# Three of four block sums moved from GpSimd to VectorE in a Strassen-like mixture-of-experts stage, with later output DMAs and a re-spaced start of the stage

## The chip, the cores and the metric

The kernel runs on one core of a Trainium2 chip. The core has five engines with a queue each: TensorE (PE, matmuls; PEld is its weight load), VectorE (DVE), ScalarE (ACT), GpSimd (POOL) and SyncE (SP, which here only issues DMAs). Every queue is worked off in order: an instruction that waits holds up all that stand behind it on its engine, and only there. The metric is the device time of one execution in microseconds (us); lower is better.

## The reference

Windowed attention, then a feed-forward block with a rational activation, then a mixture of 8 experts whose gate is normalised by 8 rounds of row and column scaling.

```python
x = attention(q, k, v)                    # (4, 8, 576, 64) -> (2304, 512)
h = x @ w_in                              # (2304, 2048)
x = rational(h, a, b) @ w_out             # (2304, 512)
logits = x @ w_gate                       # (2304, 8)
P = np.exp(logits - logits.max())
for _ in range(8):
    P /= P.sum(1, keepdims=True) + 1e-09
    P /= P.sum(0, keepdims=True) + 1e-09
    P *= N / E
for e in range(8):
    h = np.maximum(x @ w1[e], 0.0)        # w1[e]: (512, 1024)
    out += P[:, e:e + 1] * (h @ w2[e])    # w2[e]: (1024, 512)
```

## The kernel before

All arithmetic is float32 in effect: each matrix is split into a high and a low float16 part, and each product is three float16 matmuls (high-high, high-low, low-high).

The expert stage takes about two thirds of the time, and the change lies in it. Both of its matrix products are computed with seven block products in place of eight. The tokens are three groups G of 768, each of two blocks of 384. A **macro** m is one expert, one token group and one of `NP` = 4 pairs of 128 hidden columns: 8 x 3 x 4 = 96 macros. A macro's first layer is seven **units** (`moe_unit`, positions 0 to 6, position 1 seven units late), each six matmuls of 128x384. Their sums leave PSUM as they come up: positions 0, 2 and 4 by ACT copies (L973), position 3 by a DVE add (L975) and an ACT relu (L976), position 5 by a DVE add (L978), position 6 by an ACT relu (L980), position 1 by a DVE add (L983) and an ACT relu over two blocks (L984). These evacuations matter: positions 0, 2, 4 and 6 add into one PSUM bank (`l1a`), so PE may not start position 2 before L973 has read position 0, and so on; positions 3, 5 and 1 share the bank `l1b` in the same way with L975, L978 and L983.

After the four blocks of h (the tile E) come **four sums of blocks** (the tile D in room IG), written by `combine` (L946): o = 6 is E1 - E0 and needs only position 6's relu; o = 4, 5 and 7 come after L984, and 5 needs 4, and 7 needs 5. Before, a macro with m < 4 makes all four on DVE, every other macro makes all four on GpSimd. Then E[1:4] (1152 columns) and D (1536 columns) are each split: the high part by ACT (L990), the low part by DVE (L991), two of each in a macro. From here on "first" L990 or L991 is the one of E, "second" the one of D.

The second layer (`moe_l2`) lags by `LG` = 28 units; in every unit three of its products run (nine matmuls of 128x256, L1013 to L1015) between the units of the first layer. A finished piece is summed out of PSUM by one ACT copy (L1032) and seven DVE adds (L1034), scaled by the gate on ACT (L1043, twice), and added to the output in HBM by a DMA that GpSimd issues (L1048; for expert 0 SP issues a plain one).

The weights of the next expert are prepared meanwhile: loaded into two buffers by SP (L838, L844 to L846), their maximum taken on DVE (L850), four differences made on GpSimd (L873; for expert 0 on DVE), and split by ACT (L884) and DVE (L887). The gate's rounds (`gate_iter`) are nine small DVE operations and one tiny matmul that waits for them; group 2 of x is cut and stored by `mix_at` near the start of the stage.

What sets the order: the code places work at units (`at_u`, `prep_at`, `mix_at`), and a scheduler then orders each engine's queue by its own estimates. `pin` adds a dependency that keeps a GpSimd or other instruction behind the last named sum or split.

Of the kernel before, what the change touches and what calls it, by code (L numbers as in the profile page):

```python
# [16 lines left out]
ALU = mybir.AluOpType  # L17
# [11 lines left out]
def kernel(  # L29
# [14 lines left out]
    nc = tc.nc  # L44
# [199 lines left out]
    for i, x in enumerate(SEAMS):  # L244
        if x is None:
            continue
        m = masks[:, i, 0:32 + x]
# [430 lines left out]
    def rat_c(st):  # L678
        d = cur[st]
        g = d.pop("g")  # L680
        gh, gl = (slab_g[:, x + st % 2, :] for x in (0, 2))
        nc.scalar.activation(gh, g, AF.Copy)  # L682
        nc.gpsimd.tensor_tensor(out=gl, in0=g, in1=gh.bitcast(F32), op=ALU.subtract)  # L683
        d.update(gh=gh, gl=gl)
# [132 lines left out]
    NP = NF2 // 2  # L817
# [10 lines left out]
    def pin(eng, i):  # L828
        if eng in behind:
            tc.add_manual_dep(i.ins, behind[eng], mybir.DependencyInfo(mybir.DependencyClass.Sync, mybir.DependencyReason.DATA), reason="after this group's h")  # L830
# [111 lines left out]
    def combine(m, o, x, y, op):  # L942
        d = mac[m]
        a, b = (d["E"][:, z, :] if z < 4 else d["D"][:, z - 4, :] for z in (x, y))
        eng = nc.vector if m < NP else nc.gpsimd
        i = eng.tensor_tensor(out=d["D"][:, o - 4, :], in0=a, in1=b, op=op)  # L946
        if m >= NP:
            behind["p"] = i.ins.name

    def moe_unit(u):  # L950
# [41 lines left out]

    yb = {}
    pend = []
    gate_ready = [False]
    PRODS = ((0, 0, 1, 0), (0, 1, 5, 4), (1, 0, 4, 3), (1, 1, 6, 5), (2, 0, 3, 1), (2, 1, 7, 2), (3, 0, 2, 6))
    NQ = NM * 3 * 7
# [21 lines left out]
    def gate_col(e, tt):  # L1019
        if (e, "pw") not in pw:  # L1020
            pwt = cpool.tile([P, NTT], F32, tag=f"pw{e % 2}", name="pwt")
            nc.vector.tensor_scalar(out=pwt, in0=gate_t["pe"][:, e, :], scalar1=i_e[:, e % 2:e % 2 + 1], scalar2=None, op0=ALU.mult)
            pw[e, "pw"] = pwt
        return pw[e, "pw"][:, tt:tt + 1]
# [15 lines left out]
    def y_out(v, p, yd):  # L1040
        e, G = GV[v]
        for n in range(2):
            nc.scalar.activation(yd[:, n, :], yd[:, n, :], AF.Copy, scale=gate_col(e, 2 * TPB * G + TPB * n + p))  # L1043
        dst = bass.AP(out.tensor, (2 * TPB * G + p) * P * DM, [[DM, P], [TPB * P * DM, 2], [1, DM]])
        if e == 0:
            nc.sync.dma_start(out=dst, in_=yd)
        else:
            nc.gpsimd.dma_start(out=dst, in_=yd, accum_op=ALU.add)  # L1048

    def flush_pend():  # L1050
        gate_ready[0] = True
        for a in pend:
            y_out(*a)
        pend.clear()
# [57 lines left out]
    def at(s, fn, *a):  # L1112
        slots[s].append((fn, a))
# [12 lines left out]
    def at_u(u, fn, *a):  # L1126
        at(4 * NS1 + int(2 * u), fn, *a)
# [10 lines left out]
    def mix_at(G, when, s0, slot0):  # L1138
        for dt, c, slot in zip(s0, (CX00, CX10, CT1, CX11, CT2, CT3, CT4), (0, 1, 2, 3, 0, 1, 2)):
            if c in (CT1, CT2, CT3, CT4):  # L1140
                when(dt, mix_sub, G, c)
            when(dt, mix_put, G, c, slot0 + slot)
            if c == CX11:
                when(dt + (0.5 if G < 2 else 2), x2_logits, G)
# [3 lines left out]

    mix_at(0, at_step, (56, 57, 58, 59, 61, 62, 63), 0)
    mix_at(1, at_step, (69, 70, 71, 72, 74, 75, 76), 0)  # L1150
    mix_at(2, at_u, (9.5, 11, 12.5, 14, 29, 31, 33), 4)
    for c in range(7):
        at_step(78 + c // 3, x_load, 0, c)
    at_step(80.5, x_load, 1, CX00)

    at_u(20.5, gate_exp)
    for u in (23, 25.5, 31, 35, 38, 42, 45, 49):
        at_u(u, gate_iter)
    at_u(50, gate_done)
    at_u(50.5, flush_pend)  # L1160

    use = []

# [4 lines left out]
    def prep_at(s, e, k, step):  # L1168
        for n in range(4):
            at(int(s + n * step), raw_diff, e, k, n)  # L1170
        for n in range(4):
            at(int(s + (1, 2, 4, 5)[n] * step), raw_part, e, k)
        use.append((int(s + 5 * step), e, k, s))

    US = 4 * NS1
# [5 lines left out]
        prep_at(4 * x + 1, 0, i, 1)  # L1181
    for i, x in ((0, 90), (3, 92), (1, 94)):
        prep_at(4 * x + 1, 0, NP + i, 1)
    prep_at(US + 2 * 16, 0, NP + 2, 1)
    for e in range(1, NE):
        u0 = EU * (e - 1)
        for i in range(8):
# [12 lines left out]
    def run_slot(s):  # L1200
        for fn, a in slots.pop(s, ()):
            early = fn is run_piece or fn is flush
            with tc.high_priority(offset=400) if early else ExitStack():
                more = fn(*a)
            if callable(more):
                at(s + 1, more)
# [78 lines left out]
        run_slot(4 * g + 3)  # L1285
    side_mode[0] = 1
    for u in range(NU + LG):
        if u == LG:
            side_mode[0] = 2
        if u == 0:  # L1290
            rat_b(NS1 - 1)
        moe_unit(u)
        run_slot(US + 2 * u)
        if u < 2 * LAG:
            rat_l2(NS1 - LAG + u // 2, u % 2)
        if u == 1:
            rat_c(NS1 - 1)
        for q in range(3 * (u - LG), 3 * (u - LG + 1)):
            if 0 <= q < NQ:
                moe_l2(q)  # L1300
        run_slot(US + 2 * u + 1)
    assert not slots


# [28 lines left out]
```

## Time and profile before

| | us |
|---|---|
| median of 3 runs (lowest, highest) | 2087.18 (2082.1, 2087.22) |
| the profiled execution | 2087.59 |
| its span, first to last instruction | 2085.8 |
| busy in the span: PE, DVE, ACT, POOL | 1914.8, 1515.0, 1229.1, 944.9 |

A busy time is the sum over stages with different limits, and PE's matmuls are pipelined, so a busy PE is not a PE at its peak. Idle time of an engine costs the kernel something only where PE, or the end, waits for what that engine does next.

### The profile page before, as it was taken

The page shows a single profiled execution, that of the slowest core. Times are in us where ns is not written, and L with a number is a line of the kernel's source. Part 1 is how long each engine was busy: PE and PEld are TensorE (multiplying, and loading weights), DVE is VectorE, ACT ScalarE, POOL GpSimd, SP SyncE. Part 2 cuts the span into 40 slices and gives each one's busy share as a digit, 9 for nine tenths or more (in the row PEclk, how much of TensorE's full clock was granted, in tenths as well). Part 3 has the DMA queues.
Part 4 walks back from the last instruction along what each step waited for, and adds up shares of the span by engine and source line. Part 5 has one row for each costly group of instructions (what it writes and reads, how often), then busy time and mean ns, then how long its engine had stood idle before and what let it go on. Part 6 is the DMA issues. An engine that isn't in the chain of part 4 may idle for free. (4 is left out here: it accounts for less than half of the span.)

```text
span 2085.8 us, 36459 instructions
## 1 busy us (share of the span) xinstructions
PE 1914.8 (92%) x13914; PEld 1433.3 (69%) x13914; DVE 1515.0 (73%) x2572; ACT 1229.1 (59%) x2328; POOL 944.9 (45%) x846
## 2 busy tenths in 40 slices
PE   7688999998989899999999999999999999999997
PEld 6466767776766566767677677677677667767776
DVE  5898899899998776667576666666666666666653
ACT  5677777685777345545554654654555455455542
POOL 1232333221221036546564763665566476475542
PEclk7699999998999899999999999999999999999999
DMA  6542220134211251344245345345435524633323
GB/s 170 160 139 77 59 70 12 35 99 130 84 39 54 68 171 61 104 129 107 59 125 147 64 111 155 72 99 129 105 59 125 159 60 104 160 75 71 79 61 49
DMA packets 209792, 200.07 MB, mean 96 GB/s; under 512 B 78288, under 2 KB 160208, under 8 KB 209616
## 3 DMA queue, kind: packets, MB, share of 16 engines
q1 hardware_dynamic: 192480, 164.70, 26.0%
q0 software_dynamic: 17136, 33.03, 10.6%
q8 instruction: 109, 1.79, 0.4%
q14 instruction: 67, 0.55, 0.1%
HBM read 151.67 MB, written 46.01 MB: 95 GB/s over the span
## 5 line engine op out<-in xcount | busy, mean ns | idle before, releaser
L924 PEld LDWEIGHTS <-roomA 128*128 128x128 f16 x3276 | 320.9, 98 | 223.1 <-issue 59.2
L924 PE MATMUL l1a<-roomA 128*128 128x384 f16 x1872 | 358.3, 327 | 28.5 <-ACT roomA L973 16.8
L924 PE MATMUL l1b<-roomA 128*128 128x384 f16 x1404 | 274.4, 330 | 14.5 <-DVE roomV L978 5.3
L683 POOL TENSOR_TENSOR roomIG<-roomA,roomIG 128x384 fp32r<-128x384 f32 x96 | 112.5, 1172 | 290.4 <-ACT roomIG L682 222.2
L946 POOL TENSOR_TENSOR roomIG<-roomV 128x384 f32<-128x384 f32 x92 | 112.8, 1227 | 262.6 <-ACT roomV L980 112.8
L873 POOL TENSOR_TENSOR roomA<-roomA 128x256 f32<-128x256 f32 x224 | 211.2, 962 | 22.3 <-DVE roomA L887 8.4
L946 POOL TENSOR_TENSOR roomIG<-roomA 128x384 f32<-128x384 f32 x92 | 110.4, 1200 | 195.2 <-ACT roomA L980 99.4
L1013 PE MATMUL yps<-roomA 128*128 128x256 f16 x630 | 170.9, 273 | 7.0 <-ACT roomA L884 2.7
L1013 PE MATMUL yps<-roomA,roomV 128*128 128x256 f16 x630 | 171.6, 275 | 2.4 <-DVE roomA L1034 1.5
L1014 PE MATMUL yps<-roomA,roomV 128*128 128x256 f16 x630 | 172.1, 275 | 0.0
L1015 PE MATMUL yps<-roomA 128*128 128x256 f16 x630 | 170.6, 274 | 1.0 <-DVE roomA L991 1.0
L1015 PE MATMUL yps<-roomA,roomV 128*128 128x256 f16 x630 | 170.3, 275 | 1.3 <-DVE roomV L991 1.3
L1014 PE MATMUL yps<-roomA 128*128 128x256 f16 x630 | 171.4, 273 | 0.0
L645 PE MATMUL h1ps<-roomA 128*128 128x384 f16 x384 | 130.6, 341 | 16.4 <-DVE roomA L665 8.2
L991 DVE TENSOR_TENSOR roomV<-roomIG,roomV 128x1536 f16<-128x1536 f32 x48 | 87.6, 1825 | 79.2 <-ACT roomV L990 79.2
L887 DVE SCALAR_TENSOR_TENSOR roomA<-roomA,sm 128x768 f16<-128x768 f32 (+1 forms) x92 | 123.8, 1355 | 28.3 <-ACT roomA L884 27.6
L991 DVE TENSOR_TENSOR roomA<-roomIG,roomA 128x1536 f16<-128x1536 f32 x48 | 94.2, 1962 | 68.0 <-ACT roomA L990 68.0
L698 PE MATMUL o1ps<-roomIG,roomV 128*128 128x384 f32 x384 | 137.6, 358 | 4.2 <-POOL roomIG L683 4.1
L884 ACT ACTIVATE roomA<-roomA,sm 128x768 f16<-128x768 f32 (+1 forms) x92 | 94.5, 1037 | 79.7 <-POOL roomA L873 50.7
L699 PE MATMUL o1ps<-roomIG,roomV 128*128 128x384 f32 x384 | 131.3, 342 | 0.0
L646 PE MATMUL h1ps<-roomA 128*128 128x384 f16 x384 | 130.0, 339 | 0.0
L647 PE MATMUL h1ps<-roomA 128*128 128x384 f16 x384 | 129.7, 338 | 0.0
(216 smaller groups left out, 5240.9 us busy)
## 6 DMA issues: line engine op xcount, KB each, us to landing
roomA<-xd SPq DMA_DIRECT2D x119, 384.0 KB
roomA<-in_moe_w_dram SPq DMA_DIRECT2D x256, 128.0 KB
roomA<-in_moe_w_dram SPq DMA_DIRECT2D x128, 256.0 KB
out_dram<-roomV POOLq DMA_DIRECT2D x32, 512.0 KB, 5.8
out_dram<-roomA POOLq DMA_DIRECT2D x31, 512.0 KB, 6.1
roomV<-in_moe_w_in_dram SPq DMA_DIRECT2D x16, 512.0 KB
roomA<-in_moe_w_out_dram SPq DMA_DIRECT2D x16, 512.0 KB
xd<-roomA SPq DMA_DIRECT2D x14, 384.0 KB
```

The lines of the kernel that those rows point to most:

```text
L645: mm = nc.tensor.matmul(hp, whi, xb[:, 0, kk, :], start=kk == 0, stop=False)
L646: nc.tensor.matmul(hp, whi, xb[:, 1, kk, :], start=False, stop=False)
L647: nc.tensor.matmul(hp, wlo, xb[:, 0, kk, :], start=False, stop=kk == KD - 1)
L698: nc.tensor.matmul(ob[dd], hi, d["gl"], start=False, stop=False)
L699: nc.tensor.matmul(ob[dd], lo, d["gh"], start=False, stop=last)
L873: pin("p" if e else "v", eng.tensor_tensor(out=d[:, o, :], in0=a, in1=b, op=ALU.add if w == 0 and n == 0 else ALU.subtract))
L924: mm = nc.tensor.matmul(ps, w[:, wx_, wh, kk * P:(kk + 1) * P], x[:, xh, kk, :], start=start and kk == 0 and wh == 0 and xh == 0, stop=sto ...
L946: i = eng.tensor_tensor(out=d["D"][:, o - 4, :], in0=a, in1=b, op=op)
L991: behind["v"] = nc.vector.tensor_tensor(out=h[:, 1, o, :], in0=src, in1=h[:, 0, o, :], op=ALU.subtract).ins.name
L1013: nc.tensor.matmul(o, hh[:, a - 1, c], w[:, m, 0, :], start=i == 0 and half == 0, stop=False)
L1014: nc.tensor.matmul(o, hh[:, a - 1, c], w[:, m, 1, :], start=False, stop=False)
L1015: nc.tensor.matmul(o, hl[:, a - 1, c], w[:, m, 0, :], start=False, stop=i == NP - 1 and (half == 1 or b == 3))
```

## The change

Four things. `combine` puts only o = 6 on GpSimd, for every macro, and o = 4, 5 and 7 on DVE. The output DMAs on GpSimd (experts 1 to 7) are issued two units later in the program than the scaling before them, and pinned behind the last o = 6. The work at the start of the stage is placed at other units: the seven cuts of group 2, the gate's exponential (20.5 to 23.5), its eight rounds (from 23, 25.5, 31, 35, 38, 42, 45, 49 to one every three units from 26 to 47), its end and the held-back outputs, and one weight preparation of expert 0 (unit 16 to 23). Nothing else is edited, but the scheduler orders all queues anew.

```diff
--- before.py
+++ after.py
@@ -942,9 +942,9 @@
     def combine(m, o, x, y, op):
         d = mac[m]
         a, b = (d["E"][:, z, :] if z < 4 else d["D"][:, z - 4, :] for z in (x, y))
-        eng = nc.vector if m < NP else nc.gpsimd
+        eng = nc.gpsimd if o == 6 else nc.vector
         i = eng.tensor_tensor(out=d["D"][:, o - 4, :], in0=a, in1=b, op=op)
-        if m >= NP:
+        if o == 6:
             behind["p"] = i.ins.name
 
     def moe_unit(u):
@@ -992,6 +992,8 @@
 
     yb = {}
     pend = []
+    later_u = []
+    unit_now = [0]
     gate_ready = [False]
     PRODS = ((0, 0, 1, 0), (0, 1, 5, 4), (1, 0, 4, 3), (1, 1, 6, 5), (2, 0, 3, 1), (2, 1, 7, 2), (3, 0, 2, 6))
     NQ = NM * 3 * 7
@@ -1045,7 +1047,7 @@
         if e == 0:
             nc.sync.dma_start(out=dst, in_=yd)
         else:
-            nc.gpsimd.dma_start(out=dst, in_=yd, accum_op=ALU.add)
+            later_u.append((unit_now[0] + 2, lambda: pin("p", nc.gpsimd.dma_start(out=dst, in_=yd, accum_op=ALU.add))))
 
     def flush_pend():
         gate_ready[0] = True
@@ -1148,16 +1150,16 @@
 
     mix_at(0, at_step, (56, 57, 58, 59, 61, 62, 63), 0)
     mix_at(1, at_step, (69, 70, 71, 72, 74, 75, 76), 0)
-    mix_at(2, at_u, (9.5, 11, 12.5, 14, 29, 31, 33), 4)
+    mix_at(2, at_u, (9, 12, 15.5, 19, 27.5, 30, 32.5), 4)
     for c in range(7):
         at_step(78 + c // 3, x_load, 0, c)
     at_step(80.5, x_load, 1, CX00)
 
-    at_u(20.5, gate_exp)
-    for u in (23, 25.5, 31, 35, 38, 42, 45, 49):
+    at_u(23.5, gate_exp)
+    for u in (26, 29, 32, 35, 38, 41, 44, 47):
         at_u(u, gate_iter)
-    at_u(50, gate_done)
-    at_u(50.5, flush_pend)
+    at_u(49, gate_done)
+    at_u(49.5, flush_pend)
 
     use = []
 
@@ -1181,7 +1183,7 @@
         prep_at(4 * x + 1, 0, i, 1)
     for i, x in ((0, 90), (3, 92), (1, 94)):
         prep_at(4 * x + 1, 0, NP + i, 1)
-    prep_at(US + 2 * 16, 0, NP + 2, 1)
+    prep_at(US + 2 * 23, 0, NP + 2, 1)
     for e in range(1, NE):
         u0 = EU * (e - 1)
         for i in range(8):
@@ -1285,6 +1287,9 @@
         run_slot(4 * g + 3)
     side_mode[0] = 1
     for u in range(NU + LG):
+        unit_now[0] = u
+        while later_u and later_u[0][0] <= u:
+            later_u.pop(0)[1]()
         if u == LG:
             side_mode[0] = 2
         if u == 0:
@@ -1299,6 +1304,8 @@
             if 0 <= q < NQ:
                 moe_l2(q)
         run_slot(US + 2 * u + 1)
+    for _, fn in later_u:
+        fn()
     assert not slots
```

Lines from L994 on are two higher in the changed kernel, from L1048 on a few more; L1034 becomes L1036, L1043 becomes L1045, L1048 becomes L1050.

First place: DVE in the macro m = 66 (expert 5), from one second L991 to the next; roomV_6583 and roomA hold the blocks E of two macros, roomIG holds D. Before:

```order
L978 TENSOR_TENSOR roomV_6583<-l1b,roomV_6583 128x384
L850 TENSOR_REDUCE sm<-roomA 128x1 x2
L200 TENSOR_REDUCE sm<-sm 128x1
L850 TENSOR_REDUCE sm<-roomA 128x1
L983 TENSOR_TENSOR roomV_6583<-l1b,roomV_6583 128x384
L975 TENSOR_TENSOR roomA<-l1b,roomA 128x384
L991 TENSOR_TENSOR roomV_6693<-roomV_6583,roomV_6693 128x1152
L991 TENSOR_TENSOR roomV_6693<-roomIG,roomV_6693 128x1536
```

In the changed kernel:

```order
L1036 TENSOR_TENSOR roomA<-yps,roomA 128x256
L978 TENSOR_TENSOR roomV_6583<-l1b,roomV_6583 128x384
L975 TENSOR_TENSOR roomA<-l1b,roomA 128x384
L850 TENSOR_REDUCE sm<-roomA 128x1 x2
L200 TENSOR_REDUCE sm<-sm 128x1
L983 TENSOR_TENSOR roomV_6583<-l1b,roomV_6583 128x384
L850 TENSOR_REDUCE sm<-roomA 128x1
L946 TENSOR_TENSOR roomIG<-roomV_6583 128x384
L991 TENSOR_TENSOR roomV_6693<-roomV_6583,roomV_6693 128x1152
L946 TENSOR_TENSOR roomIG<-roomIG,roomV_6583 128x384
L946 TENSOR_TENSOR roomIG<-roomV_6583,roomIG 128x384
L991 TENSOR_TENSOR roomV_6693<-roomIG,roomV_6693 128x1536
```

L978 and L975 now stand ahead of the maxima L850, L983 stands ahead of the third L850 where it stood behind it, and the three sums stand one ahead of the first L991 and two behind it.

The same macro on ACT, before:

```order
L1043 ACTIVATE roomA<-roomA,pwt 128x512 x2
L973 ACTIVATE roomV_6583<-l1a 128x384
L973 ACTIVATE roomA<-l1a 128x384
L980 ACTIVATE roomV_6583<-l1a 128x384
L984 ACTIVATE roomV_6583<-roomV_6583 128x768
L973 ACTIVATE roomA<-l1a 128x384
L990 ACTIVATE roomV_6693<-roomV_6583 128x1152
L976 ACTIVATE roomA<-roomA 128x384
L990 ACTIVATE roomV_6693<-roomIG 128x1536
```

In the changed kernel:

```order
L973 ACTIVATE roomA<-l1a 128x384
L973 ACTIVATE roomV_6583<-l1a 128x384
L1045 ACTIVATE roomA<-roomA,pwt 128x512 x2
L976 ACTIVATE roomA<-roomA 128x384
L980 ACTIVATE roomV_6583<-l1a 128x384
L984 ACTIVATE roomV_6583<-roomV_6583 128x768
L990 ACTIVATE roomV_6693<-roomV_6583 128x1152
L973 ACTIVATE roomA<-l1a 128x384
L990 ACTIVATE roomV_6693<-roomIG 128x1536
```

Both have the second L990 at the end with an L973 between L984 and it; the next macro's L973 stands behind it in both.

Second place: GpSimd at the end of macro 64, in 65 and at the start of 66. Before:

```order
L946 TENSOR_TENSOR roomIG<-roomIG,roomV_6583 128x384
L946 TENSOR_TENSOR roomIG<-roomV_6583,roomIG 128x384
L1048 DMA out_dram<-roomV_6583 128x2x512
L946 TENSOR_TENSOR roomIG<-roomA 128x384 x2
L946 TENSOR_TENSOR roomIG<-roomIG,roomA 128x384
L946 TENSOR_TENSOR roomIG<-roomA,roomIG 128x384
L1048 DMA out_dram<-roomA 128x2x512
L946 TENSOR_TENSOR roomIG<-roomV_6583 128x384 x2
```

In the changed kernel, where a macro fills one row, macros 64 to 68:

```order
L1050 DMA out_dram<-roomA 128x2x512
L873 TENSOR_TENSOR roomA<-roomA 128x256 x4
L946 TENSOR_TENSOR roomIG<-roomV_6583 128x384
L1050 DMA out_dram<-roomV_6583 128x2x512
L946 TENSOR_TENSOR roomIG<-roomA 128x384
L1050 DMA out_dram<-roomA 128x2x512
L946 TENSOR_TENSOR roomIG<-roomV_6583 128x384
L946 TENSOR_TENSOR roomIG<-roomA 128x384
L1050 DMA out_dram<-roomV_6583 128x2x512
L946 TENSOR_TENSOR roomIG<-roomV_6583 128x384
```

A macro has one sum in place of four, and an output DMA stands between sums as before, two units later.

Third place: DVE in the macro m = 3, the last before the second layer begins; gt and gs are the gate's tiles, smps its tiny matmul's. Before:

```order
L787 TENSOR_REDUCE gs<-gt 128x18
L946 TENSOR_TENSOR roomIG<-roomA 128x384 x2
L788 TENSOR_SCALAR gs<-gs 128x18
L946 TENSOR_TENSOR roomIG<-roomIG,roomA 128x384
L789 RECIPROCAL gs<-gs 128x18
L975 TENSOR_TENSOR roomA<-l1b,roomA 128x384
L946 TENSOR_TENSOR roomIG<-roomA,roomIG 128x384
L790 TENSOR_TENSOR gt<-gt,gs 128x144
L792 TENSOR_REDUCE gs<-gt 128x8
L991 TENSOR_TENSOR roomA<-roomIG,roomA 128x1536
```

In the changed kernel, its first twelve rows:

```order
L787 TENSOR_REDUCE gs<-gt 128x18
L873 TENSOR_TENSOR roomA<-roomA 128x256 x2
L887 SCALAR_TENSOR_TENSOR roomA<-roomA,sm 128x3x256
L946 TENSOR_TENSOR roomIG<-roomA 128x384
L788 TENSOR_SCALAR gs<-gs 128x18
L873 TENSOR_TENSOR roomA<-roomA 128x256
L946 TENSOR_TENSOR roomIG<-roomIG,roomA 128x384
L789 RECIPROCAL gs<-gs 128x18
L873 TENSOR_TENSOR roomA<-roomA 128x256
L975 TENSOR_TENSOR roomA<-l1b,roomA 128x384
L946 TENSOR_TENSOR roomIG<-roomA,roomIG 128x384
L790 TENSOR_TENSOR gt<-gt,gs 128x144
```

One sum has left, and four differences and one split of expert 0's weights have come in ahead of L975.

## Rows read from the trace of the kernel before

**Rows 1.** Stretches: busy us (count) of PE, PEld, DVE, ACT, POOL; PEclk, DMA, GB/s.

```profile
676.00:704.00 28.00, 17.61 (x82) 9.75 (x82) 25.03 (x50) 14.10 (x21) 0.00 (x0) 0.71 0.41 127
760.00:840.00 80.00, 75.02 (x558) 55.17 (x556) 55.91 (x84) 44.44 (x64) 47.84 (x41) 0.98 0.30 94
840.00:1956.00 1116.00, 1063.27 (x8020) 783.20 (x8018) 732.48 (x1025) 607.41 (x884) 658.57 (x564) 1.00 0.43 106
```

**Rows 2.** Waits of PE, 840 to 1956: waited for, us in total, times, longest.

```profile
PE l1a L924 <- ACT roomA L973: 15.6, 18, 2.3
PE l1a L924 <- ACT roomV L973: 13.6, 22, 0.9
PE l1b L924 <- DVE roomV L978: 6.9, 8, 0.9
PE yps L1013 <- DVE roomA L1034: 5.4, 10, 0.9
PE yps L1013 <- DVE roomV L1034: 4.2, 7, 0.9
PE yps L1013 <- ACT roomA L884: 2.7, 5, 0.6
```

**Rows 3.** Timeline around macro 66: start, us, operation, [idle before <- releaser].

```profile
1631.15 1.22 DVE L850 TENSOR_REDUCE sm<-roomA 128x1 f32<-128x1024 f32 x1 [5.58 <-DMA roomA<-in_moe_w_dram]
1633.62 0.47 ACT L973 ACTIVATE roomA<-l1a 128x384 f32<-128x384 f32 x1
1637.97 1.48 ACT L990 ACTIVATE roomV<-roomIG 128x1536 f16<-128x1536 f32 x1 [2.41 <-POOL roomIG L946]
1639.36 0.47 ACT L973 ACTIVATE roomA<-l1a 128x384 f32<-128x384 f32 x1
1634.87 1.00 POOL L946 TENSOR_TENSOR roomIG<-roomIG,roomV 128x384 f32<-128x384 f32 x1
1635.95 1.99 POOL L946 TENSOR_TENSOR roomIG<-roomV,roomIG 128x384 f32<-128x384 f32 x1
1634.15 1.14 PE L924 MATMUL l1a<-roomA 128*128 128x384 f16 x6 [2.33 <-ACT roomA L973]
1639.88 1.79 PE L924 MATMUL l1a<-roomA 128*128 128x384 f16 x10 [0.90 <-ACT roomA L973]
```

**Rows 4.** Groups: DVE 650 to 700; DVE, then POOL, 840 to 1956: busy, mean ns.

```profile
L991 DVE TENSOR_TENSOR roomV<-roomV,roomV 128x1152 f16<-128x1152 f32 x2 | 2.7, 1349 | 0.0
L946 DVE TENSOR_TENSOR roomIG<-roomV 128x384 f32<-128x384 f32 x4 | 2.2, 552 | 0.9 <-ACT roomV L984 0.9
...
L887 DVE SCALAR_TENSOR_TENSOR roomA<-roomA,sm 128x768 f16<-128x768 f32 (+1 forms) x72 | 98.6, 1379 | 24.5 <-ACT roomA L884 24.1
L991 DVE TENSOR_TENSOR roomV<-roomV,roomV 128x1152 f16<-128x1152 f32 x26 | 53.4, 2052 | 37.7 <-ACT roomV L990 37.0
...
L873 POOL TENSOR_TENSOR roomA<-roomA 128x256 f32<-128x256 f32 x204 | 192.0, 960 | 20.6 <-DVE roomA L887 7.2 <-DMA roomA<-in_moe_w_dram 5.8 <-DVE roomV L887 2.2
L946 POOL TENSOR_TENSOR roomIG<-roomV 128x384 f32<-128x384 f32 x77 | 94.8, 1231 | 152.7 <-ACT roomV L980 88.7 <-ACT roomV L984 64.0
L946 POOL TENSOR_TENSOR roomIG<-roomV,roomIG 128x384 f32<-128x384 f32 x38 | 69.7, 1835 | 3.0
L1048 POOL DMA_DIRECT2D out_dram<-roomV x27 | 32.5, 1204 | 61.2 <-ACT roomV L1043 57.5 <-DVE roomA L991 3.5
```

**Rows 5.** Timeline of PE: five waits outside the steady part.

```profile
691.33 2.08 PE L924 MATMUL l1b<-roomA 128*128 128x384 f16 x6 [1.72 <-DVE roomV L975]
696.58 2.08 PE L924 MATMUL l1b<-roomA 128*128 128x384 f16 x6 [3.18 <-DVE roomA L975]
702.90 0.60 PE L173 MATMUL smps<-gs,sm 128*128 128x8 f32 x2 [4.02 <-DVE gs L792]
755.79 1.78 PE L924 MATMUL l1b<-roomA 128*128 128x384 f16 x6 [2.98 <-DMA roomA<-xd]
2056.29 0.39 PE L1015 MATMUL yps<-roomA 128*128 128x256 f16 x2 [0.96 <-DVE roomA L991]
```

## The prediction, made before the changed kernel was run

> **What bounds the kernel now.** I read the stretches first [rows 1]. From 840 to 1956 us, with no special work, PE is busy for 1063.27 of 1116 us at the full clock (PEclk 1.00), so 52.7 us is all that a better order can win there; from 760 to 840 it is 5.0 us. The rest of the expert stage looks alike but for its first microseconds: from 676 to 704 PE is busy for 17.61 of 28 us at a granted clock of 0.71, while DVE is busy for 25.03. So PE is the bound, and the first microseconds belong to DVE.
>
> Second, who holds PE up [rows 2]. Of the 52 us, 29.2 (15.6 + 13.6, 40 waits of 0.73 us in the mean) are waits for L973, the ACT copy after positions 0, 2 and 4; 6.9 are for L978 on DVE; 9.6 for L1034 on DVE; 2.7 for the weight split L884; a few small rows make up the rest. None names GpSimd. But L973 is half a microsecond of work, so it is late because of what stands ahead of it on ACT.
>
> Third, one macro in the order of time [rows 3]. The second L990 starts at 1637.97 after ACT stood idle for 2.41 us waiting for GpSimd's last sum; L973 behind it starts at 1639.36; PE starts at 1639.88, after 0.90 us of waiting. The last sum took 1.99 us where the one before took 1.00. The larger wait here, 2.33 us at 1634.15, has another root: DVE stood for 5.58 us at a maximum (L850) whose weights had not landed, with L983 behind it, L984 behind that on another engine, and L973 behind L984.
>
> **The sums.** A sum on GpSimd takes 1.23 us in the mean for one form and 1.84 for the last of the four; on DVE, with GpSimd at rest, 0.552 [rows 4]. In the changed kernel DVE does sum 4, the first L991 (1.349 at rest) and sums 5 and 7 between the end of L984 and the start of the second L990: 3 x 0.552 + 1.349 = 3.0 us. Before, the three took about 1.08 + (1637.94 - 1634.87) = 4.15 us, where 1.08 is the spacing of the two starts in [rows 3] taken for the first sum too. So the second L990 can start 1.15 us earlier, more than the mean wait of 0.73 for an L973 and more than the 0.9 for an L978 that stands behind the second L991.
>
> What it costs: 77 macros in the steady part x 3 x 0.552 = 127.5 us more on DVE, from 732.48 to at most 860 of 1116 us (66% to 77%). Against it stands what DVE loses beside GpSimd today: the first L991 takes 2.052 us in [rows 4] and 1.349 at rest, and most of GpSimd's sums go. I leave this saving out of the load and take it as cover.
>
> The Trainium skill, page "SBUF — State Buffer", section "Who interferes with whom", says that a DVE instruction with two SBUF inputs contends with a GpSimd instruction that reads SBUF, and that the one that starts first keeps the other out until it is done; the trace agrees, with 1.99 us for a sum of 1.00 and 2.052 for an L991 of 1.349. That speaks against the change, since the moved sums have two SBUF inputs too: GpSimd keeps 204 differences of 0.96 us and 77 sums of 1.23, 290 of 1116 us, so by this rule (an estimate of mine) 231 sums would meet one in a quarter of the cases and lose half a microsecond each, 30 us more on DVE, and the total would come out some 2 us higher than mine.
>
> Line by line for the steady part:
> - L973, 29.2 us. Those behind the second L990 go, by the 1.15 us. The large one at L850 goes as well, because L983 now stands ahead of the third L850 (first place in the section on the change). Others stand behind L884 or behind L984, and after the large wait goes PE reaches the next L973 sooner. I keep a quarter: -22, between -29 and 0.
> - L978 and the small rows for L991, 9 us of the waits. Gone by the 1.15 us, except that in one macro of twelve L978 now stands behind three splits L887 of 1.38 us each: -7, between -9 and +3.
> - L1034 and L884, some 13 us: unchanged in the sum. GpSimd has more time for the differences that L884 waits for, but DVE is fuller.
> - Given back: 9.6 us are waits for DVE adds today, at 34% idle; at 23% idle they would be about half as long again: +4, between 0 and +40 (see the slow rival).
>
> Sum: -25.
>
> **The output DMA, two units later.** Issuing one takes GpSimd 1.2 us, and it stood 61.2 us in all at 27 of them waiting for ACT's scaling L1043 [rows 4], with sums behind it. With the sums gone, only the differences and sum 6 stand behind it. Its landing is not waited for: two output tiles alternate and a piece takes over nine units, so two units of delay are covered. Cost nothing; the gain is in the lines above. If that cover failed, L1034 would wait.
>
> **The start of the stage.** Four of PE's waits of 676 to 704 stand in the trace; I quote three [rows 5]: 1.72 and 3.18 us for L975 and 4.02 for the gate's second round. In the changed kernel only one round stands ahead of the second layer, so the 4.02 us lie beside matmuls. Two sums have left DVE's queue, and one wide split (at most 1.38) now comes behind L792: up to 2.5 us. But four differences (each below a sum's 0.552) and a split (1.38) have moved to just ahead of the last L975 and L792 (third place): up to 3.5 us later there, less what was taken away before. I take -2, between -6.5 (4.02 + 2.5) and +2. Seven loads of x now come ahead of second-layer weights on SP; the 2.98 us at 755.79 waits for such a load. I take half: -1.5, between -3 and 0. From 760 to 840: the steady share, 25 / 52.7 of 5.0, -2.3.
>
> **The end.** The last wait for L991, 0.96 us [rows 5], goes with the sums; the last DMA itself waits for ACT, as before: -1.
>
> Total: -25 - 2 - 1.5 - 2.3 - 1 = -31.8. The profiled execution took 2087.59, 0.4 above the median of 2087.18, so the forecast is **2056 us**. About 0.3%, or 6.3 us, is what a measurement of this kernel can tell from no change.
>
> **Rivals.**
> - More: every wait for L973, L978 and L991 goes, the start gains 6.5, the load 3, the end 1, and 760 to 840 gains 4: 2087.6 - 29 - 9 - 6.5 - 3 - 1 - 4 = 2035. For it: the 1.15 us exceeds each typical wait. Against: some L973 stand behind L884. Chance 0.10.
> - Half given back: the sums take DVE when PE needs L1034, L975 or L978, and half of the 31.8 returns: 2072. For it: L1034 and L978 already cost 17 us at 66% busy. Chance 0.20.
> - The change does not reach PE: the waits for L973 trace back to L887 and L850 on DVE, as the 2.33 us did, rather than to GpSimd; something else is then last, and the time stays within 6 us of 2087. Against: the 2.41 us of ACT idle before the second L990. Chance 0.12.
> - Slower: the first sum waits at the head of DVE's queue for L984, and evacuations stand behind it. The pace is 1116 / 77 = 14.5 us a macro, 2.07 a unit. L975 has about one unit to spare, L978 two. Waiting for L984, three sums and the first L991 take up to 3.0 + 1.4 (the first L991's present wait, 37.0 / 26) = 4.4 us, so it decides where an L975 falls due inside them. If half of the 92 macros lost 0.9 us there, that is 41 us against some 20 still won: 2108. Against: the first L991 stands there today and waits in the same way. The lock in the page named above would work in the same direction. Chance 0.16.
> - The forecast itself, 2046 to 2066: 0.42.
>
> **Chances and range.** Forecast, more and half given back are faster: 0.72; no effect: 0.12; slower: 0.16. The range of 2034 to 2094 leaves out little of the first rival and most of the slow one, under 0.2. The likeliest case alone is 2046 to 2066.
>
> **What the new profile would show.** Sums at L946 on DVE near 0.55 to 0.7 us, 276 moved; the first L991 nearer 1.35 than 2.05; ACT's wait of 2.41 before the second L990 replaced by one under 2 for DVE; PE's waits for L973 in 840 to 1956 near 7 us rather than 29; no smps wait of 4 us before the second layer. The forecast is wrong if PE's waits for L975, L978 and L1034 grow by more than 10 us together, or if waits for L973 remain above 20 with L850 or L887 ahead of them.

## The result, and the profile after

The changed kernel takes **2048.25 us** in the median (2047.18 to 2050.52) against 2084.64 of before on the same chip: a ratio of 0.983, 95% interval [0.981, 0.985]. The forecast was 2056, with a range of 2034 to 2094. By the medians the gain is 36.4 us. The profiled execution took 2048.93, 38.7 less than the one of before.

Where the 38.7 us are is read by landmarks: the starts of L984 of macros 0, 15 and 93 in ACT's timeline (660.0, 881.3 and 2021.1 us before, 662.9, 882.3 and 1982.5 after). Up to macro 0, ahead of any change, the changed kernel loses 2.9 (over the fourteen kernels of this document that start lies between 657.8 and 665.0 us, so this is what two executions differ by); from 0 to 15 it gains 1.9; from 15 to 93, the steady part, 39.6; from there to the end 0.1. The steady part alone gives the whole gain.

The windows of before over that steady part (columns as in [rows 1]):

```profile
881.30:2021.10 1139.80, 1087.07 (x8211) 801.79 (x8208) 742.70 (x1042) 616.10 (x898) 666.24 (x568) 1.00 0.43 104
```

And of the changed kernel, with two stretches of the start that answer to [rows 1]:

```profile
676.00:704.00 28.00, 20.37 (x136) 12.65 (x137) 27.20 (x45) 16.11 (x22) 3.29 (x2) 0.79 0.48 164
760.00:840.00 80.00, 74.75 (x548) 54.47 (x547) 67.47 (x113) 48.52 (x70) 25.39 (x26) 0.94 0.32 104
882.30:1982.50 1100.20, 1077.36 (x8195) 802.16 (x8194) 844.38 (x1271) 615.42 (x894) 322.81 (x332) 1.00 0.44 107
```

The steady part went from 1139.8 to 1100.2 us. PE's idle time fell from 52.7 to 22.8, some 30 us; the other 10 come from a *busy* PE, 1077.4 in place of 1087.1, though both kernels issue 13914 matmuls in all (16 fewer fall into the second window, some 2 us of the 10). POOL's busy time halved, DVE's rose by 102 us.

PE's waits in the steady part of the changed kernel, which answer to [rows 2]:

```profile
PE l1a L924 <- ACT roomA L973: 5.9, 6, 2.3
PE yps L1015 <- ACT roomA L884: 3.8, 4, 1.5
PE yps L1016 <- DVE roomA L887: 3.3, 4, 0.8
PE yps L1015 <- DVE roomA L1036: 2.1, 6, 0.4
PE l1a L924 <- ACT roomV L973: 2.1, 6, 0.4
PE yps L1015 <- ACT roomV L884: 1.8, 2, 1.0
PE yps L1016 <- DVE roomV L887: 1.6, 2, 0.8
PE yps L1015 <- DVE roomV L1036: 1.4, 4, 0.4
```

The waits for L973 fell from 29.2 to 8.0; those for L978 and L991 are gone; those for L887 are new, once in an expert; those for L884 rose from 3.7 to 5.6.

DVE's groups of the same stretch, which answer to [rows 4]:

```profile
L991 DVE TENSOR_TENSOR roomV<-roomV,roomV 128x1152 f16<-128x1152 f32 x26 | 35.2, 1353 | 0.3
L946 DVE TENSOR_TENSOR roomIG<-roomIG,roomA 128x384 f32<-128x384 f32 x39 | 35.9, 922 | 1.3
L946 DVE TENSOR_TENSOR roomIG<-roomA 128x384 f32<-128x384 f32 x39 | 27.7, 711 | 29.5 <-ACT roomA L984 29.5
L946 DVE TENSOR_TENSOR roomIG<-roomV 128x384 f32<-128x384 f32 x39 | 27.4, 702 | 24.4 <-ACT roomV L984 24.4
L946 DVE TENSOR_TENSOR roomIG<-roomIG,roomV 128x384 f32<-128x384 f32 x39 | 24.1, 618 | 0.9
L946 DVE TENSOR_TENSOR roomIG<-roomA,roomIG 128x384 f32<-128x384 f32 x39 | 22.0, 564 | 0.2
L946 DVE TENSOR_TENSOR roomIG<-roomV,roomIG 128x384 f32<-128x384 f32 x39 | 21.5, 552 | 0.4
```

The form of the first L991 shown here (26 of 78) is at 1353 ns, its time at rest (2052 before); the other three forms are at 1492, 2015 and 1359, so the mean of all is 1.51 us, against 1.88 before over the same stretch. The sums cost 552 ns at best and 922 in one form. All six forms together are 158.6 us for 234 sums, 0.68 each, 29 us above 234 times 0.552.

Macro 66 in the order of time, which answers to [rows 3]:

```profile
1600.60 0.84 ACT L984 ACTIVATE roomV<-roomV 128x768 f32<-128x768 f32 x1 [2.50 <-DVE roomV L983]
1606.00 1.22 DVE L850 TENSOR_REDUCE sm<-roomA 128x1 f32<-128x1024 f32 x1 [5.43 <-DMA roomA<-in_moe_w_dram]
1607.14 0.55 DVE L946 TENSOR_TENSOR roomIG<-roomV 128x384 f32<-128x384 f32 x1
1607.60 1.35 DVE L991 TENSOR_TENSOR roomV<-roomV,roomV 128x1152 f16<-128x1152 f32 x1
1609.46 0.56 DVE L946 TENSOR_TENSOR roomIG<-roomV,roomIG 128x384 f32<-128x384 f32 x1
1610.11 1.48 ACT L990 ACTIVATE roomV<-roomIG 128x1536 f16<-128x1536 f32 x1 [7.09 <-DVE roomIG L946]
1611.50 0.47 ACT L973 ACTIVATE roomA<-l1a 128x384 f32<-128x384 f32 x1
1612.02 1.17 PE L924 MATMUL l1a<-roomA 128*128 128x384 f16 x6 [2.25 <-ACT roomA L973]
```

The maximum L850 still waits 5.43 us for its weights. L983 now stands ahead of it, as the order promised, but the first sum stands behind it, so the second L990 waits 7.09 us in place of 2.41, and PE waits 2.25 for L973 (2.33 before). This wait has moved by one instruction and costs the same.

The prediction's measure of the second L990, ACT's idle time just before it, before:

```profile
L990 ACT ACTIVATE roomA<-roomIG 128x1536 f16<-128x1536 f32 x39 | 57.8, 1483 | 67.2 <-POOL roomIG L946 66.7
L990 ACT ACTIVATE roomV<-roomIG 128x1536 f16<-128x1536 f32 x39 | 57.6, 1477 | 61.5 <-POOL roomIG L946 61.5
```

and after:

```profile
L990 ACT ACTIVATE roomA<-roomIG 128x1536 f16<-128x1536 f32 x39 | 57.9, 1483 | 64.7 <-DVE roomIG L946 64.7
L990 ACT ACTIVATE roomV<-roomIG 128x1536 f16<-128x1536 f32 x39 | 57.8, 1481 | 70.1 <-DVE roomIG L946 70.1
```

128.2 us before (for 78), 134.8 after: by this row nothing became shorter. Idle time starts when ACT has finished other work, so it is the wrong measure. Taken from the end of L984 to the start of the second L990, from ACT's timeline between 870 and 1960 us, the mean is 4.75 us before (74 pairs found) and 3.99 after (77). This interval is called the **run to L990** below.

At the start of the stage, DVE and PE:

```profile
694.69 1.75 DVE L887 SCALAR_TENSOR_TENSOR roomA<-roomA,sm 128x768 f16<-128x768 f32 x1
698.75 1.76 PE L924 MATMUL l1b<-roomA 128*128 128x384 f16 x5 [6.67 <-DVE roomA L975]
...
757.42 1.22 DVE L850 TENSOR_REDUCE sm<-roomA 128x1 f32<-128x1024 f32 x1 [2.98 <-DMA roomA<-in_moe_w_dram]
758.55 0.16 DVE L191 TENSOR_SCALAR gs<-l1b 128x8 f32<-128x8 f32 x1
758.76 1.24 PE L924 MATMUL l1b<-roomA 128*128 128x384 f16 x6 [3.40 <-DVE gs L191]
765.54 2.08 PE L924 MATMUL l1a<-roomA 128*128 128x384 f16 x6 [2.81 <-ACT roomV L973]
```

PE waits 6.67 us for an L975 that stands behind expert 0's differences and splits (one of 1.75 us ahead of it). Sixty microseconds later a maximum L850 waits 2.98 us for weights; L191, which reads a gate round's tiny matmul out of the bank l1b, stands behind it on DVE, and PE cannot use the bank for 3.40 us. A wait of 2.81 follows.

### The profile page after: what moved, and what is told of

The parts are those of the page before. It is cut to its first block, busy times and chain, and to the rows that moved or that the text cites. A ratio compares the mean times of both kernels' runs of the same rounds, so it can differ in the third digit from the quotient of the medians.

```text
span 2047.1 us, 36511 instructions
## 1 busy us (share of the span) xinstructions
PE 1904.1 (93%) x13914; PEld 1433.2 (70%) x13914; DVE 1635.2 (80%) x2844; ACT 1230.9 (60%) x2328; POOL 551.0 (27%) x574
## 3 DMA queue, kind: packets, MB, share of 16 engines
q8 instruction: 109, 1.79, 0.4%
## 5 line engine op out<-in xcount | busy, mean ns | idle before, releaser
L924 PEld LDWEIGHTS <-roomA 128*128 128x128 f16 x3276 | 322.1, 99 | 199.4 <-issue 36.5
L873 POOL TENSOR_TENSOR roomA<-roomA 128x256 f32<-128x256 f32 x224 | 198.3, 912 | 104.5 <-DVE roomA L887 62.2
L698 PE MATMUL o1ps<-roomIG,roomV 128*128 128x384 f32 x384 | 137.9, 359 | 5.2 <-POOL roomIG L683 4.9
L946 POOL TENSOR_TENSOR roomIG<-roomA 128x384 f32<-128x384 f32 x48 | 57.1, 1190 | 313.8 <-ACT roomA L980 235.1
L699 PE MATMUL o1ps<-roomIG,roomV 128*128 128x384 f32 x384 | 131.4, 342 | 0.0
L887 DVE SCALAR_TENSOR_TENSOR roomA<-roomA,sm 128x768 f16<-128x768 f32 (+1 forms) x92 | 118.0, 1300 | 10.8 <-ACT roomA L884 8.0
L697 PE MATMUL o1ps<-roomIG,roomV 128*128 128x384 f32 x384 | 107.7, 382 | 16.3 <-ACT roomIG L682 14.6
L1016 PEld LDWEIGHTS <-roomA 128*128 128x128 f16 x1008 | 98.6, 98 | 30.5 <-issue 7.4
L884 ACT ACTIVATE roomA<-roomA,sm 128x768 f16<-128x768 f32 (+1 forms) x92 | 93.5, 1036 | 43.6 <-POOL roomA L873 18.9
L1015 PEld LDWEIGHTS <-roomA 128*128 128x128 f16 x1008 | 98.6, 98 | 29.5 <-issue 6.3
```

Source lines behind the costliest of these rows:

```text
L698: nc.tensor.matmul(ob[dd], hi, d["gl"], start=False, stop=False)
L699: nc.tensor.matmul(ob[dd], lo, d["gh"], start=False, stop=last)
L873: pin("p" if e else "v", eng.tensor_tensor(out=d[:, o, :], in0=a, in1=b, op=ALU.add if w == 0 and n == 0 else ALU.subtract))
L887: pin("v", nc.vector.scalar_tensor_tensor(out=l, in0=x, scalar=sc, in1=h, op0=ALU.mult, op1=ALU.subtract))
L924: mm = nc.tensor.matmul(ps, w[:, wx_, wh, kk * P:(kk + 1) * P], x[:, xh, kk, :], start=start and kk == 0 and wh == 0 and xh == 0, stop=sto ...
L1015: nc.tensor.matmul(o, hh[:, a - 1, c], w[:, m, 0, :], start=i == 0 and half == 0, stop=False)
```

## The experiments

Twelve kernels. Every ratio is to the kernel before, run on the same chip; the chips differ between the groups of runs, so medians of different groups compare best by their ratios. The two stretches are worked out from the starts of L984 of macros 0, 15 and 87 in ACT's timeline of one execution; the last column is the run to L990. The stretch from 15 to 87 repeats well: the four kernels that have both the moved sums and the later DMAs lie between 1019.0 and 1019.4.

| kernel | median us | ratio, 95% interval | 0 to 15 | 15 to 87 | run |
|---|---|---|---|---|---|
| before | 2084.6 to 2088.1 | | 221.3 | 1057.2 | 4.75 |
| changed | 2048.3 | 0.983 [0.981, 0.985] | 219.4 | 1019.4 | 3.99 |
| sums alone | 2037.5 | 0.976 [0.974, 0.977] | 213.0 | 1015.0 | 3.92 |
| output DMAs alone | 2091.2 | 1.002 [1.001, 1.003] | 221.7 | 1060.0 | 4.78 |
| start alone | 2086.1 | 0.999 [0.998, 1.000] | 219.1 | 1056.0 | 4.75 |
| sums and DMAs | 2040.9 | 0.977 [0.976, 0.978] | 213.1 | 1019.2 | 3.98 |
| sums alone, GpSimd busy late | 2164.8 | 1.036 [1.034, 1.037] | 236.7 | 1111.6 | 5.70 |
| sums alone, GpSimd busy early | 2137.6 | 1.024 [1.021, 1.026] | 230.2 | 1100.8 | 5.30 |
| sums alone, ahead of L991 | 2019.1 | 0.966 [0.965, 0.968] | 214.6 | 999.8 | 2.51 |
| sums and differences on DVE | 2007.5 | 0.961 [0.959, 0.962] | 210.9 | 991.4 | 3.15 |
| changed, preparation at 16 | 2049.7 | 0.982 [0.981, 0.984] | 223.6 | 1019.1 | 3.99 |
| changed, gate as before | 2040.9 | 0.978 [0.977, 0.979] | 214.6 | 1019.0 | 4.00 |
| both of the two best | 2007.6 | 0.962 [0.961, 0.963] | 210.6 | 993.1 | 2.48 |
| all on DVE | 2001.8 | 0.959 [0.957, 0.960] | 209.4 | 990.1 | 2.38 |

**1 to 4. The parts of the change.** Each is the diff shown above, cut to that part: `combine` alone; `later_u` alone; the unit numbers alone; `combine` with `later_u`.

Sums alone: 

> Only the sums are moved (three of four on VectorE, o = 6 on GpSimd for every macro); output DMAs and the start of the stage as before. Chain theory (the gain is the shorter run of work from L984 to the second L990): nearly all of the 36 us, so about 2052 us (2046 to 2058), PE's waits for L973 in the steady part 6 to 12 us in place of 29. DMA theory (GpSimd's waits at the output DMA, with sums behind them, held the second L990): sum 6 still stands behind an output DMA that waits for L1043, so only about half, near 2066 us, with ACT waiting for sum 6 before the second L990. Start theory (much of the gain is from the re-spaced start): 2060 us or more, and the steady part alone as in the changed kernel.

Output DMAs alone: 

> Only the output DMAs are issued two units later and pinned behind o = 6's place (here behind the last sum on GpSimd); sums and start as before. Chain theory: four sums stay on GpSimd and the run from L984 to the second L990 is as long as before, so 2085 us within 6. DMA theory: GpSimd no longer stands 57 us in all at the output DMA with sums behind it, so 15 to 20 us are gained, near 2067 us.

Start alone: 

> Only the start of the stage is placed anew (cuts of group 2, the gate's rounds, one weight preparation). By the prediction 2 us for the start and 1.5 for the load of x, less what the changed kernel shows in new waits (6.67 us for L975 and 3.40 us for the gate's tile): between -4 and +4 us, so 2085 us within 5, and the steady part as before (about 52 us of idle PE). Start theory: 2075 us or less.

Sums and output DMAs: 

> Sums and output DMAs as in the changed kernel, the start of the stage as before. If the new start is worth nothing, 2048 us within 4; if the new waits at the start (6.67 and 3.40 us) are a price of it, 2042 us; if it is worth the 3.5 us of the prediction, 2052 us. Against the run with the sums alone: the same within 4 us if the output DMA costs nothing, as predicted; 10 us or more below it by the DMA theory.

The sums alone gain 50 us, more than any theory said and more than the whole change. The DMA theory falls: the later DMAs gain nothing alone and cost 2.8 us from macro 15 to 87, and beside the sums they cost 4.2 there (3.4 by the medians, whose intervals overlap). The new start gains 2 us alone, hardly more than its interval can tell from nothing, and costs 6.3 from macro 0 to 15 beside the sums (219.4 against 213.1).

How a later DMA costs: the orders of ACT and DVE are the same with the sums alone and with the DMAs too, and only GpSimd's differs. PE's waits for L884 in the steady part are 0.8 us with the sums alone and 5.0 with the DMAs too:

```profile
PE yps L1015 <- ACT roomA L884: 3.0, 3, 1.5
PE yps L1015 <- ACT roomV L884: 2.0, 2, 1.1
```

At one of them the timeline of the kernel with sums and DMAs has

```profile
1894.29 1.04 DVE L946 TENSOR_TENSOR roomIG<-roomA 128x384 f32<-128x384 f32 x1 [0.67 <-ACT roomA L984]
1894.85 3.55 POOL L873 TENSOR_TENSOR roomA<-roomA 128x256 f32<-128x256 f32 x4
1895.37 2.44 DVE L946 TENSOR_TENSOR roomIG<-roomIG,roomA 128x384 f32<-128x384 f32 x1
```

and at the same place the kernel with the sums alone has

```profile
1887.94 0.86 DVE L946 TENSOR_TENSOR roomIG<-roomA 128x384 f32<-128x384 f32 x1 [0.67 <-ACT roomA L984]
1888.25 5.00 POOL L873 TENSOR_TENSOR roomA<-roomA 128x256 f32<-128x256 f32 x4
1888.83 1.03 DVE L946 TENSOR_TENSOR roomIG<-roomIG,roomA 128x384 f32<-128x384 f32 x1
```

One of the two trains gives way. With the DMAs late, four differences run at their pace (3.55 us) and a sum of 0.55 takes 2.44; with the sums alone the differences take 5.00 and the sum 1.03. Over the steady part this form of the sum takes 886 ns with the DMAs and 747 without. At this place ACT waits 4.34 us for the sums before the second L990, against 3.25 with the sums alone. L884 stands behind it, and PE waits 1.54 us for L884 in place of 0.35. What the DMAs cost alone was not followed up.

**5, 6. GpSimd busy again.** On the kernel with the sums alone:

```diff
+            for n, (x, y) in enumerate(((0, 2), (1, 0), (3, 1))):
+                nc.gpsimd.tensor_tensor(out=spare, in0=E[:, x, :], in1=E[:, y, :], op=ALU.add)
```

stands behind the three sums; in the second kernel it stands behind sum 6, with E1 and E0 three times. The result is read by nothing.

Late: 

> The kernel with only the sums moved (2037.5 us against 2088.0 of before), and beside it three more additions of 128x384 on GpSimd in every macro, behind the three sums on VectorE: they read the blocks E that those sums read, wait for the same L984, and write a tile that nobody reads. GpSimd is then about as busy as before (some 60%), at the same moments. Quiet theory (the gain is that GpSimd no longer works beside the first L991 and the sums, which then run at 0.55 and 1.35 us): 2065 us or more, the sums at L946 on DVE well over 0.8 us in the mean. Chain theory (the gain is that the three sums no longer pass through GpSimd, whatever else GpSimd does): 2037 to 2050 us.

Early: 

> The same three additional additions in every macro, but placed behind sum 6 (they need L980 only), so that most of them lie ahead of L984 and beside other work of DVE. Theory of the place (only what DVE meets between L984 and the second L990 counts): 2037 to 2046 us. Quiet theory for all of DVE (every operation of DVE beside GpSimd's gets longer, and at 77% busy that reaches PE): 2060 us or more, about as much as with the late ones.

Both are slower than before, by 127 and 100 us against the sums alone, though nothing reads the additional work's result; the waits of ACT for it, where L973 writes a block E anew, come to 1.9 and 0.7 us in the steady part. DVE's groups of the late one (L947 and L994 are L946 and L991, two to three lines lower):

```profile
L994 DVE TENSOR_TENSOR roomV<-roomV,roomV 128x1152 f16<-128x1152 f32 x24 | 45.2, 1881 | 0.0
L947 DVE TENSOR_TENSOR roomIG<-roomA 128x384 f32<-128x384 f32 x36 | 54.8, 1522 | 24.4 <-ACT roomA L985 24.3
L947 DVE TENSOR_TENSOR roomIG<-roomIG,roomA 128x384 f32<-128x384 f32 x36 | 39.6, 1100 | 1.2
```

Three lines of it: sums of 1.1 and 1.5 us and a first L991 of 1.88. The sums on DVE are here nearly as slow as GpSimd's were [rows 4]. The theory of the place is not settled by the early ones: by the trace 1.6 of their 3.6 us a macro still lie between L984 and the second L990 (late 3.5 of 4.2), and the run to L990 is 5.30 with them. Part of the loss may be GpSimd's own queue: ACT's waits for the differences ahead of L884 go from 19.7 us with the sums alone to 29.2 (late) and 31.8 (early), and PE's waits for L884 from 0.8 to 4.6 and 10.5. But before the change ACT waited 61.5 us there, twice as long in a kernel that is 77 us faster than the late one, so earlier differences are not the main gain of the moved sums either. No wait before the second L990 ends with sum 6. And PE's granted clock in the steady part is 0.99 (late) and 0.98 (early) in place of 1.00. The shares were not separated.

**7. The sums ahead of the first L991.** On the sums alone, GpSimd as it was there:

```diff
+        else:
+            behind["s"] = i.ins.name
...
-                behind["v"] = nc.vector.tensor_tensor(out=h[:, 1, o, :], in0=src, in1=h[:, 0, o, :], op=ALU.subtract).ins.name
+                lo = nc.vector.tensor_tensor(out=h[:, 1, o, :], in0=src, in1=h[:, 0, o, :], op=ALU.subtract)
+                pin("s", lo)
+                behind["v"] = lo.ins.name
```

> The kernel with only the sums moved, and all three sums on DVE ahead of the first L991 (in place of one ahead and two behind it in most macros). If the run of work from L984 to the second L990 is still what costs, the second L990 comes about 1.35 us earlier (its wait for L946 falls from about 1.9 us to about 0.8), and 3 to 8 us are gained: 2030 to 2035 us. If the chain no longer costs PE anything (its 9 us of waits for L973 come from late weights), 2037 us within 3. If L991 and what stands behind it now come late, 2042 us or more.

18 us are gained (15 of them from macro 15 to 87), two to six times what was expected. The pin is the only edit, but the scheduler answered it with another order on ACT too (some 300 of its 2328 instructions stand elsewhere), so the gain is not shown to come from DVE's order alone. ACT's second splits (L992 is L990):

```profile
L992 ACT ACTIVATE roomV<-roomIG 128x1536 f16<-128x1536 f32 x39 | 57.8, 1482 | 6.1 <-DVE roomIG L946 5.8
L992 ACT ACTIVATE roomA<-roomIG 128x1536 f16<-128x1536 f32 x39 | 57.7, 1479 | 13.9 <-DVE roomIG L946 12.7
```

18.5 us of waits for the sums in place of 129.6 with the sums alone. So the run to L990 was still worth 18 us when PE's waits for L973 showed 9.

**8. The differences on DVE too.** On the sums alone:

```diff
-        eng = nc.gpsimd if e else nc.vector
-        pin("p" if e else "v", eng.tensor_tensor(out=d[:, o, :], in0=a, in1=b, op=ALU.add if w == 0 and n == 0 else ALU.subtract))
+        eng = nc.vector
+        pin("v", eng.tensor_tensor(out=d[:, o, :], in0=a, in1=b, op=ALU.add if w == 0 and n == 0 else ALU.subtract))
```

> The kernel with only the sums moved, and the four differences of each weight (L873, 196 in the steady part, 0.95 us each on GpSimd) on DVE as well, so that GpSimd keeps only sum 6 and the output DMAs. Theory of the shared access (DVE's and GpSimd's operations hold each other up: sums of 0.55 that take 0.7 to 1.0): DVE gets some 75 us more work (0.37 us each), but loses part of it again, the splits L884 and L887 come earlier, PE's waits for L887 (5 us) go: 2030 to 2037 us. Load theory (DVE at 77% has no room): DVE goes to 83%, PE waits for L978, L983 and L1034 grow by more than 10 us: 2047 us or more.

30 us are gained, more than either theory said. The steady part of the sums alone, then of this kernel:

```profile
872.10:1966.80 1094.70, 1076.51 (x8194) 802.08 (x8193) 839.07 (x1271) 615.40 (x895) 329.53 (x332) 1.00 0.46 108
```

```profile
869.30:1939.60 1070.30, 1069.21 (x8198) 802.53 (x8197) 864.49 (x1470) 623.43 (x895) 156.40 (x136) 1.00 0.46 110
```

199 more instructions on DVE, the differences at 0.47 us each, add only 25 us to its busy time, since the others fall back to their times at rest: from 840 to 1880 us all six forms of the sum are at 552 to 557 ns, and the split L887 of 128x1024 goes from 1477 to 1282. PE is busy for 1069.2 of 1070.3 us.

**9, 10. The start, part by part.** On the changed kernel: `prep_at(US + 2 * 23, ...)` back to 16; and the gate's rounds at 25, 27, 31, 35, 38, 42, 45, 49 with its end at 50 and the held-back outputs at 50.5.

Preparation: 

> The changed kernel with the one weight preparation of expert 0 back at unit 16 (from 23), all else of the new start kept. The changed kernel stands at 0.983 of before, the sums and output DMAs with the old start at 0.977: some 6 to 12 us are lost at the new start. Theory of the preparation (four differences and a split of expert 0, 3.3 us, stand on DVE ahead of the last L975, for which PE waits 6.67 us): that wait falls to 2 us or less, and 4 to 6 us come back, 0.980 of before or less. Theory of the gate (the round at unit 47 is what costs): 0.983 as before, and the wait of 6.67 us, if it goes, comes back at another place of the start.

Gate: 

> The changed kernel with the gate's rounds from the second on, its end and the held-back outputs back at the units of before (first round at 25), all else of the new start kept. Theory of the gate (a round's tiny matmul is placed in a bank of the first layer, its reader L191 stands on DVE behind a maximum L850 that waits for its weights, and PE waits 3.40 us for it, then 0.65 and 2.81): these three waits go, and 4 to 7 us come back, 0.980 of before or less. Theory of the preparation: 0.983 as before.

The preparation is not what costs: with it back at 16 the kernel is no faster. PE's timeline with it at 16:

```profile
696.45 1.14 PE L924 MATMUL l1b<-roomA 128*128 128x384 f16 x6 [3.33 <-DVE roomV L975]
702.07 0.59 PE L173 MATMUL smps<-gs,sm 128*128 128x8 f32 x2 [4.48 <-DVE gs L792]
```

The 6.67 us are now 3.33 and 4.48 at two places, and the three waits behind the gate's round are there as before (3.80, 0.65 and 2.82). With the gate's rounds put back these three go, the 6.67 stays, and 7 us come back (by the ratios 10; from macro 0 to 15, 4.8). The window behind the gate, which answers to the one of the changed kernel above, has 603 matmuls at a granted clock of 1.00, where that had 548 at 0.94:

```profile
760.00:840.00 80.00, 78.26 (x603) 58.78 (x602) 68.75 (x111) 48.64 (x69) 25.65 (x26) 1.00 0.30 99
```

**11, 12. Together.** Experiments 7 and 8 in one, and then sum 6 on DVE too.

Both: 

> The sums moved, all three ahead of the first L991, and the differences L873 on DVE too; output DMAs and start of the stage as before. Each alone gave 2019 and 2007.5 us. PE was busy for 1069 of 1070 us in the steady part with the differences alone on DVE, so nothing is left there: 2007 us within 3. If busy PE still hides stalls that an earlier second L990 takes away, 2003 us or less.

All on DVE: 

> As the kernel with both, and sum 6 on DVE as well, so that GpSimd does no arithmetic in the steady part and only issues output DMAs. Shared access: no operation of DVE meets one of GpSimd any more, all at their times at rest (0.55 for a sum, 1.75 for the second L991): 2007 us within 4, since PE is the bound. Load theory: DVE gets some 40 us more (about 84% busy), PE waits for DVE's evacuations again: 2015 us or more.

Both together are no better than the differences alone, since PE was at its bound. With sum 6 on DVE as well the steady part is

```profile
867.50:1936.00 1068.50, 1068.30 (x8191) 801.41 (x8190) 895.02 (x1547) 625.59 (x894) 69.89 (x58) 1.00 0.46 110
```

and the whole 2001.8 us, the fastest kernel of the study: 46 us below the changed one (by the ratios 50), and below the 2003 to 2011 that the theory of the shared access gave. Of the 5 us between the two profiled executions of this kernel and the differences alone, 2 are in the steady part, 1.5 at the start and 1.5 at the end. DVE is at 84%, and PE does not wait for it.

## Why the prediction was right, and where it was not

**Right in direction and near in size:** the steady part was forecast at -25 and came at -39.6. L973: -22 forecast, -21.2 by the rows. L978 and L991: -7 forecast, -9.7. L1034 and L884 unchanged: 13.3 before, 9.1 after. Given back, +4: it was to be longer waits for DVE's adds, but those for L1034 fell from 9.6 to 3.5; 4.9 came as waits for L887, which the prediction does not name, so this term fits by luck. That the total lies within 8 us of the forecast is in part luck too: the sums alone gained 50 us, some 19 more than everything in the forecast, and the other two parts, put at nothing and at a gain, took back 11.

**The step that failed first: "52.7 us is all that a better order can win there".** With all on DVE the steady part takes 1068.5 us, 71.3 below before, and PE's busy time is 1068.3 where it was 1087.1. So some 16 to 19 us of the busy PE of before (20 matmuls fewer in the window are worth 3) were stalls that the profile counts as work, and the 8 to 10 of them that the change won are most of what the steady part gained beyond the forecast. Where they lie can be worked out from [rows 3]: six matmuls of 128x384 take 1.14 us and ten 1.79, so an unhindered one starts 0.16 us after the one before, but the record of one lasts 0.33 (1.14 less five times 0.16). A wait is counted from the end of the last record only, so some 0.16 us of each stand as work. From the starts of all matmuls in the steady part of before, 83 gaps hide 13.6 us in this way, and 42 stalls too short to leave a gap hide 3.7; with all on DVE it is 0.2 and nothing.

**The 1.15 us by which the second L990 was to come earlier** are 0.76 in the mean (4.75 to 3.99). Over the kernels that leave the differences on GpSimd the run orders the time from macro 15 to 87: 5.70, 5.30, 4.75, 3.92 and 2.51 us go with 1112, 1101, 1057, 1015 and 1000. That the run sets the time is supported by experiment 7, where the pin shortens it and GpSimd's work is the same, but ACT's order changed with it; that GpSimd's work lengthens it is shown by 5, 6 and 8. The run is not all: with the differences on DVE it is 3.15, longer than in 7, and the time is shorter (991). There PE's waits for L887, 4.1 us in 7, are gone; why was not followed up.

**"The large one at L850 goes as well" failed.** It is 2.25 us, as before: the wait for the weights now holds a sum in place of L983, and ACT's wait at that place, which was to be under 2, is 7.09. There is one such wait in each of six experts: 7.6 us together before, 5.9 after. L973's rows came out right because the others went almost wholly, from 21.6 to 2.1.

**What the neighbour costs** was sized at 30 us more on DVE and 2 us of time. The 29 us are in the groups above. The Trainium skill, page "SBUF — State Buffer", section "Who interferes with whom", gives the rule by which a DVE instruction with two SBUF inputs and a GpSimd instruction that reads SBUF keep each other out; the trace agrees, and shows more than the wait for one instruction (2.44 us for a sum of 0.55 beside four differences of 0.89 each). The time was undersized, perhaps by ten: taking the differences away from GpSimd gained 30 us, though this also made the differences themselves twice as fast and reordered the queues, which was not separated. The term left out that the sums' share of it falls into the run to L990.

**"Cost nothing" for the output DMA failed, if by little.** The cover named, two output tiles that alternate, held: PE's waits for L1034's adds are 3.5 us with and without the later DMAs. The price, 3.4 us by the medians and 4.2 from macro 15 to 87, is by the rows above the meeting of differences and sums, read at one place and from the mean of one form.

**The start, the load and 760 to 840** were to gain 5.8 and gained 1.9. The sums alone gain 8.3 there. The wait for x (2.98) went, but a gate round moved behind a late L850. Of the 6.3 us lost beside the sums, 4.8 came back with the gate's old units; the rest was not traced. The +2 of the range allowed too little for a step that moves a round of the gate among maxima that wait for DMAs.

**The end** gained nothing: L991's last wait is 0.96 us, as before, and from macro 93 to the last instruction it is 64.6 us against 64.7.

The rivals: the slow one (evacuations behind the first sum) does not show, with no wait of PE for L975 or L978 in the steady part of the changed kernel. "More" is where the sums alone ended (2037.5 against 2035), though not by its way: waits for L973 of 8.6 us were still there.

## What to carry to other kernels

Moving work from GpSimd to VectorE can pay twice: the moved work is faster there, and what VectorE did beside GpSimd gets faster too; before leaving half of it on GpSimd, try none. Count the interval from the producer's end to the consumer's start, not the consumer's idle time, and do not take busy TensorE as the floor: compare the starts of successive matmuls with those of an unhindered stretch. Measure a bundle of edits part by part: here the other two took back some 11 us (by the ratios 15) of the 50 that the first had won.

## What the runs showed that was not expected

Three additional GpSimd additions in a macro, read by nothing, cost 100 to 127 us of 2038, 1.0 to 1.3 us for each macro. Sums take up to 1.5 us in the mean there against 0.55 at rest. And 13914 matmuls were 1914.8 us of busy TensorE in one kernel and 1889.4 in another, at granted clocks of 0.967 and 0.970 over the span; in the steady part, at 1.00 in both, the stalls under the records make up 17 of the 19 us between them.
